# One load moved ahead of two selects, eight small loads moved behind a memset: the start of a fused attention and feed-forward kernel

## The chip, the cores and the metric

The kernel runs on one core of a Trainium2 chip. A core has five engines that work side by side, each through its own queue in order: TensorE (PE in the profile; its weight loads are PEld), VectorE (DVE), ScalarE (ACT), GpSimd (POOL) and SyncE (SP, which only issues DMAs here). ACT, POOL and SP can issue DMAs; the transfers themselves run on 16 DMA engines. The metric is the device time of one execution in microseconds, the median of several runs.

## The reference

Two steps follow one another. The first is causal attention with a window of 128 positions and 4 sink positions that every query sees; the second is a layer norm and a two-layer feed-forward net with a residual. The inputs q, k, v have the shape (4, 8, 768, 64) in float32, the weights 512 x 2048 and 2048 x 512; the output is (4, 768, 512) in float32.

```python
scores = scale * np.matmul(q, k.transpose(0, 1, 3, 2))
keep = is_sink | in_window            # pos < 4, or 0 <= q_pos - k_pos < 128
a = softmax(np.where(keep, scores, -1e9))
x = heads_side_by_side(np.matmul(a, v))          # (4, 768, 512)
xn = (x - mu) / np.sqrt(var + 1e-06) * g_ln
out = x + np.maximum(xn @ w_ch1, 0.0) @ w_ch2
```

## The kernel before, in words

The 3072 rows are 24 tiles of 128 rows; two tiles are a chunk, so there are 12 chunks, three for each of the four batches. For each chunk the kernel loads q and k, brings them into transposed form (`kq`), computes scores, takes the exponential on ACT, masks, multiplies with v (`vn`), normalises on VectorE (`rec`, `x`, `st`, `xc`), transposes `xc` into `xnt`, and runs the two layers on PE (lines 873 and 880 for the first, 911 and 960 for the second).

The order of the work is not written out by hand and not left to a scheduler at run time. Every operation is recorded with `P.op(name, engines, priority, emit, ...)`; `Plan.run` (lines 113 to 195) goes through them with an assumed duration for each, and the result, sorted by planned start, is the order in which the instructions are emitted on every engine. `prio` decides among operations that are ready; `nb` is a time before which an operation isn't planned. Neither is a wait on the chip: there an engine takes its next instruction as soon as the semaphores of the data it reads or overwrites allow. Behind the plan, lines 1061 to 1080 fill gaps that the plan leaves on PE in the first 24 us with matmuls of a tile named `junk`, which keep PE busy and whose results nobody reads (line 1085).

The constants are recorded with `constant(...)`. The ones that matter here: `idf0` and `up0` are memsets on VectorE of `ident_f` and `upper`; `idf1` and `up1` are two `affine_select` instructions on POOL (lines 460 and 463) that make the identity and the triangle of them. VectorE then casts `ident` (466), makes `neg` from the triangle (492 to 494), and `sel`, `pick` and `mask` (498 to 507). `neg` is what PE adds into the scores of tiles 0 and 1 in place of a mask (line 701); `ident` is what PE transposes with. `vc0` (497) fills `vc`, a constant for the sinks' v.

The loads at the start:
- chunk 0, tile 0: q and k, four DMAs in float32 into `n4a`, issued by SP and ACT (line 593). VectorE and ACT cast them (610), PE transposes (622), ACT and VectorE evict into `kq` (568).
- chunk 0, tile 1: k and q, one DMA each, issued by POOL (line 599), transposed by PE (618).
- after these, on POOL's queue: v of tile 0 (562), k and q of chunk 1 into `n4b` (575), v of tile 1, and the four quarters of the first layer's weights (529) with further v loads between them; then chunk 2 into `n4c` and the second layer's weights (532).
- the sinks' v of all batches: eight DMAs of 4 KB each, one for each head, issued by SP (line 517) into 4 partitions each of `vc`. They read nothing, and write into `vc` after `vc0` has filled it. VectorE makes `vs` of it for the batches 1 to 3 (line 521); batch 0 gets its `vs` in another way (lines 676 and 679).
- g_ln, one small DMA on SP (509).

POOL issues a DMA in about 0.7 to 1 us of its own time, and takes the next instruction of its queue only then. Eight DMAs of POOL can be under way; the ninth waits for the first.

PE transposes chunk 1 from `n4b` in line 645, VectorE and ACT evict it (568).

Of the kernel before, what the change touches and what calls it, by code (L numbers as in the profile page):

```python
# [64 lines left out]
class Plan:  # L65
# [47 lines left out]
    def run(self):  # L113
# [8 lines left out]
        while ready:  # L122
# [5 lines left out]
            for o in ready:  # L128
                if "PE" in o.engs and o is not head and o.prio >= PAR["strict"]:
                    continue  # L130
# [67 lines left out]
def pe(us):  # L198
    return {"PE": (us, us + Plan.PE_DRAIN)}
# [12 lines left out]
def fix(occ, extra=0.09):  # L212
    return (occ, occ + extra)
# [12 lines left out]
NEG = -1e30  # L226
NEVER = -1e9

PAR = dict(split=(3, 4, 5, 6, 7), gsum=-8.0, guard=183.0, strict=40.0, win=0.4, tr=-8.0, sc=-5.3, sc1=-2.0, av=2.0, trx=9.0, by_dma=4, x_by_dma=2, g_on_w=2, av2=20.0, avi=1.0, behind=5, gtt=9.0, ramp=0.3, vs0=2.6, vpb=12.0,
           w1p=(0.15, 1.7, 2.05, 2.8), pm=2, w2p=(4.5, 4.51, 4.52, 4.53), by_tile=2, wino=2, vp=(0.0, 0.1, 2.0, 2.1, 4.2, 4.3), ld1=0.05)  # L230


# [129 lines left out]
def kernel(  # L362
# [59 lines left out]
    def const(name, shape, dtype):  # L422
        return consts.tile(shape, dtype, name=name)
# [6 lines left out]
    vc = const("vc", [128, B, 65], FP32)  # L430
# [15 lines left out]
    Bc = {n: Buf(n) for n in names}  # L446
# [5 lines left out]
    def constant(name, eng, us, prio, emit, reads=(), **kw):  # L452
        return P.op(name, {eng: fix(us)}, prio, emit, reads=[Bc[r] for r in reads], **kw)

    V, G = nc.vector, nc.gpsimd
# [1 line left out]
    constant("up0", "DVE", 0.13, -98, lambda e: V.memset(upper, 1.0), writes=[Bc["upper"]])  # L457
    constant("junk", "DVE", 0.28, -97, lambda e: V.memset(junk, 0.0), writes=[Bc["junk"]])
    constant("tab0", "DVE", 0.06, -96, lambda e: V.memset(one_e, 1.0), writes=[Bc["tab"]])
    constant("idf1", "POOL", 0.3, -99, lambda e: G.affine_select(  # L460
        out=ident_f, in_=ident_f, compare_op=ALU.not_equal, fill=1.0, base=0,
        pattern=[[-1, 128]], channel_multiplier=1), rw=[Bc["ident_f"]])
    constant("up1", "POOL", 0.3, -98, lambda e: G.affine_select(
        out=upper, in_=upper, compare_op=ALU.is_ge, fill=0.0, base=0,
        pattern=[[1, 128]], channel_multiplier=-1), rw=[Bc["upper"]])
    constant("idb", "DVE", 0.2, -90, lambda e: V.tensor_copy(ident, ident_f), ["ident_f"], writes=[Bc["ident"]])
# [1 line left out]
         rw=[Bc["tab"]])  # L468
# [22 lines left out]
    def negs(e):  # L491
# [14 lines left out]
    constant("ones_f", "DVE", 0.06, 7.0, lambda e: V.memset(ones_f, 1.0), writes=[Bc["ones_f"]])  # L506
    constant("masks", "DVE", 0.8, 6.0 if PAR["pm"] == 4 else -20.0, masks, ["upper"], writes=[Bc["mask"]], nb=20.0 if PAR["pm"] == 4 else 0.0)

# [3 lines left out]
    P.op("gtt", pe(0.06), 0.62, lambda e: nc.tensor.transpose(pg.t[:, 0:NDM], g4, ident_f[0:NDM, 0:NDM]),  # L512
         reads=[Bc["g4"], Bc["ident_f"]], writes=[pg], nb=PAR["gtt"])
    P.op("gt", {"DVE": fix(0.08)}, 0.63, lambda e: V.tensor_copy(gt, pg.t[:, 0:NDM]), reads=[pg], writes=[Bc["gt"]])
    for h in range(H):
        p0 = 32 * (h // 2) + NS * (h % 2)
        P.op(f"vcd{h}", {"SP": (0.3, 0.3)}, 3.2 + 0.01 * h, lambda e, h=h, p0=p0: nc.sync.dma_start(
            vc[p0:p0 + NS, :, 0:64], v[:, h, 0:NS, :].rearrange("b s d -> s b d")),
            reads=[Bc["vc"]], writes=[Bc["vcd"]], dma=HW_T, nb=30.0)
# [5 lines left out]

    w1prio = PAR["w1p"]
    for c in range(4):
# [3 lines left out]
    for c in range(4):  # L531
        P.op(f"w2ld{c}", {"POOL": (0.75, 0.8)}, PAR["w2p"][c], lambda e, c=c: G.dma_start(
            w2[c], moe_w_ch2[512 * c:512 * (c + 1), :].rearrange("(t p) n -> p t n", p=128)),
            writes=[Bw2[c]], dma=SW_W)

    def at(c, step):
        return 16.0 * c - 8.0 + PAR[step]

# [590 lines left out]
```

## Time and profile before

Median of three runs: 210.94 us (210.87 to 211.26). The profiled execution is one of its own: 211.71 us, of which the profile shows a span of 210.2 us.

| | us |
|---|---|
| median of the runs | 210.94 |
| profiled execution, span | 211.71, 210.2 |
| PE busy | 203.0 (97% of the span) |
| VectorE busy | 162.2 (77%) |
| ACT busy | 114.1 (54%) |
| POOL busy | 83.5 (40%) |
| first select on POOL starts | 1.36 |
| first load on POOL starts | 1.86 |
| PE starts on chunk 1's transposes | 12.85 |

A line of the profile names an engine, a line of the kernel, and what is written from what. In a timeline or a chain each row begins with the start in microseconds from the beginning of the span and the length; brackets hold the idle time of the engine just before, and what ended it. "SPq" is SyncE's queue of DMAs. In the list of loads the last column is the median time from issue to landing. Busy PE is not PE at its peak, since matmuls overlap.

### The profile page before, as it was taken

What the parts mean: (1) busy time and instruction counts of PE and PEld (TensorE: products, weight loads), DVE (VectorE), ACT (ScalarE), POOL (GpSimd) and SP (SyncE); (2) the same over time, 40 slices, a digit from 0 to 9 for tenths busy, and PEclk for the clock granted to TensorE, in tenths of its full rate; (3) what the DMA queues carried; (4) which work ended last, traced back from release to release, by engine and by line L of the source; (5) the groups of instructions that cost most, each with busy time, mean ns of one, the idle gap of its engine ahead of it and who ended that gap; (6) DMA issues with size and microseconds to landing.
All of it is one profiled execution on the core that took longest, in us unless ns stands there. A gap on an engine that the chain in (4) does not pass through costs nothing.

```text
span 210.2 us, 6259 instructions
## 1 busy us (share of the span) xinstructions
PE 203.0 (97%) x2539; PEld 167.9 (80%) x2544; DVE 162.2 (77%) x410; ACT 114.1 (54%) x168; POOL 83.5 (40%) x126
## 2 busy tenths in 40 slices
PE   6978999999999999999999999999999999999994
PEld 2657997764787997997987987987988988988883
DVE  5579759999688688798687797797787786797353
ACT  2559479837564564564556555554457457450620
POOL 7967583369058057058066066066020020020000
PEclk9999999999999999999999999999999999999999
DMA  5999999999999949939959939939954520220202
GB/s 115 156 198 191 199 191 208 189 173 154 212 167 127 172 109 136 188 78 120 166 122 150 174 79 156 172 77 151 177 100 53 150 53 3 100 50 4 103 30 83
DMA packets 101243, 27.51 MB, mean 131 GB/s; under 512 B 89556, under 2 KB 99032, under 8 KB 101208
## 3 DMA queue, kind: packets, MB, share of 16 engines
q0 software_dynamic: 67712, 13.37, 77.7%
q1 hardware_dynamic: 33208, 13.41, 35.5%
q8 instruction: 21, 0.34, 0.7%
q10 hardware_dynamic: 288, 0.26, 0.4%
q14 instruction: 14, 0.11, 0.2%
HBM read 27.30 MB, written 6.29 MB: 160 GB/s over the span
## 4 chain that ended last, share of the span: by engine, by line
PE 90%; DMA 3%; DVE 3%; POOL 2%; issue 0%; DVEq 0%
PE one L880 33%; PE one L960 30%; PE one L873 7%; PE one L911 7%; PE pair L805 5%; PE pair L763 4%; DMA n4b<-in_q_dram 3%; PE pair L800 2%; PE one L645 1%; POOL nat L599 1%; PE one L767 1%; DVE xnt L857 1%; DVE kq L568 1%; POOL vn L562 0%; DVE st L824 0%
## 5 line engine op out<-in xcount | busy, mean ns | idle before, releaser
L890 ACT ACTIVATE hq<-one 128x512 bf16<-128x512 f32 x92 | 55.0, 597 | 55.7 <-PE one L880 46.7
L880 PE MATMUL one<-xnt,w 128*128 128x256 bf16 x640 | 74.5, 273 | 0.0
L880 PEld LDWEIGHTS <-w 128*128 128x128 bf16 x640 | 61.4, 98 | 7.0
L777 ACT ACTIVATE pe<-pair 128x1024 bf16<-128x1024 f32 (+1 forms) x40 | 36.2, 960 | 23.2 <-PE pair L763 19.0
L832 POOL TENSOR_SCALAR st<-st 128x1 f32<-128x1 f32 x24 | 6.2, 259 | 88.2 <-DVE rec L818 74.6
L960 PEld LDWEIGHTS <-hs 128*128 128x128 bf16 x320 | 30.0, 98 | 5.2 <-DVE tm L974 0.3
L974 DVE TENSOR_TENSOR tm<-one,x 128x256 f32<-128x256 f32 x40 | 16.9, 422 | 12.3 <-PE one L960 12.3
L781 DVE TENSOR_TENSOR pe<-pe,mask 128x1024 bf16<-128x1024 bf16 (+1 forms) x40 | 24.9, 644 | 1.0 <-ACT pe L777 0.8
L960 PEld LDWEIGHTS <-hq 128*128 128x128 bf16 x240 | 23.5, 98 | 2.7
L562 POOL DMA_DIRECT2D vn<-in_v_dram x24 | 21.8, 922 | 2.0 <-DMA w<-in_moe_w_ch_dram 1.1
L943 DVE TENSOR_TENSOR hs<-hq 128x512 bf16<-128x512 bf16 x40 | 15.4, 413 | 5.3 <-ACT hq L890 5.2
L960 PE MATMUL one<-w,hq 128*128 128x256 bf16 x160 | 19.1, 273 | 0.0
L981 DVE TENSOR_TENSOR ot<-one,tm 128x256 f32<-128x256 f32 x40 | 16.7, 418 | 1.1 <-PE one L960 0.9
L820 DVE TENSOR_TENSOR x<-pair,rec 128x512 bf16<-128x512 f32 x24 | 16.6, 691 | 0.8
L824 DVE BATCH_NORM_STATS2 st<-x 128x6 f32<-128x512 bf16 x24 | 16.6, 692 | 0.5
L873 PE MATMUL one<-xnt,w 128*128 128x128 bf16 x256 | 16.3, 219 | 0.5 <-DVE xnt L857 0.5
L873 PEld LDWEIGHTS <-w 128*128 128x128 bf16 x256 | 14.7, 98 | 1.6 <-issue 0.5
L659 POOL DMA_DIRECT2D nat<-in_k_dram x16 | 15.0, 938 | 2.5 <-DMA w<-in_moe_w_ch_dram 2.5
L659 POOL DMA_DIRECT2D nat<-in_q_dram x16 | 14.2, 898 | 3.4 <-DMA w<-in_moe_w_ch_dram 3.4
L833 POOL TENSOR_TENSOR st<-st,mhalf 128x1 f32<-128x1 f32 x24 | 14.2, 592 | 2.0
L911 PE MATMUL one<-w,hq 128*128 128x512 bf16 x60 | 14.8, 380 | 0.2
L805 PE MATMUL pair<-vn,pe 128*128 128x65 bf16 x352 | 14.6, 193 | 0.0
(113 smaller groups left out, 245.1 us busy)
## 6 DMA issues: line engine op xcount, KB each, us to landing
out_dram<-ot SPq DMA_DIRECT2D x17, 256.0 KB
w<-in_moe_w_ch_dram POOLq DMA_DIRECT2D x8, 512.0 KB, 12.6
vn<-in_v_dram POOLq DMA_DIRECT2D x24, 128.0 KB, 7.2
nat<-in_k_dram POOLq DMA_DIRECT2D x17, 128.0 KB, 4.8
nat<-in_q_dram POOLq DMA_DIRECT2D x17, 128.0 KB, 5.3
out_dram<-ot SPq DMA_DIRECT2D x14, 128.0 KB
kq<-nat SPq DMA_TRANSPOSE x32
xnt<-xc SPq DMA_TRANSPOSE x20
```

What stands on the lines that cost most here:

```text
L562: P.op(f"vld{t}", {"POOL": (0.87, 0.9)}, prio, lambda e: G.dma_start(bv.t[:, :, 0:64], v[b, :, 128 * r:128 * (r + 1), :].rearrange("h p d ...
L659: lambda e, nat=nat, ap=ap: G.dma_start(nat.t, ap), writes=[nat], dma=SW, after=behind(c))
L777: P.op(f"ex{c}{hp}", {"ACT": act(2 * n)}, d + 0.1 + 0.05 * j, lambda e, pp=pp, pb=pb: nc.scalar.activation(pb.t[:, :, 0:n], pp.t[:, :, 0:n ...
L781: V.tensor_mul(pb.t[:, :, 0:n], pb.t[:, :, 0:n], mm),
L805: nc.tensor.matmul(po.t[:, h // 4, 65 * (h % 4):65 * (h % 4) + 65], lhsT=part(h, n), rhs=vn_b[tv].t[:, h, :], start=(not R and h % 4 == 0 ...
L873: nc.tensor.matmul(ph.t[:, 128 * s:128 * s + 128], lhsT=w1[u // 2][:, j, 128 * s:128 * s + 128], rhs=xnt.t[:, j, 128 * (u % 2):128 * (u % ...
L880: nc.tensor.matmul(ph.t[:, 256 * s:256 * s + 256], lhsT=w1[ht // 4][:, j, 128 * (ht % 4):128 * (ht % 4 + 1)], rhs=xnt.t[:, j, :], start=j ...
L890: nc.scalar.activation(hg.t[:, u % 4, :], ph.t, AF.Relu)
L911: nc.tensor.matmul(pc.t[:, 0:wd], lhsT=(hq[s // 2].t[:, (2 * s + i) % 4, 128 * ii:128 * ii + 128] if by_tile else hq[ht // 8].t[:, ht // 2 ...
L960: nc.tensor.matmul(at(r), lhsT=get(left, g)[:, v, s, :], rhs=rhs, start=first and n == 0, stop=n == 7, skip_group_check=True)
L974: return P.op(f"tm{name}_{c}", {"DVE": dve(256, 1.14)}, pr, lambda e: V.tensor_tensor(tm[name].t, at(r), xs[i].t[:, sl], op=ALU.add), read ...
L981: return P.op(f"o{c}_{half}", {"DVE": dve(256, 1.14)}, pr, lambda e: V.tensor_tensor(ots[i].t[:, sl], at(r), tm[name].t, op=ALU.add), read ...
```

## The change

Two constants on POOL, the identity's and the triangle's select, get a later priority, so that the plan puts the k load of tile 1 ahead of them on POOL's queue. The q load of tile 1 and all else on POOL stay behind them. A new constant `vc1` on VectorE sets one column of `vc` for batch 0 to zero (it is zero already, and nobody reads it). It is planned for 26 us at the earliest. Since it writes `vc`, the eight sink loads, which write `vc` too and are recorded behind it, wait for it on SP.

```diff
-PAR = dict(split=(3, 4, 5, 6, 7), ...
+PAR = dict(idf=-49.95, vc1=7.0, vc1nb=26.0, split=(3, 4, 5, 6, 7), ...
...
-    constant("idf1", "POOL", 0.3, -99, lambda e: G.affine_select(
+    constant("idf1", "POOL", 0.3, PAR["idf"], lambda e: G.affine_select(
         out=ident_f, in_=ident_f, compare_op=ALU.not_equal, fill=1.0, base=0,
         pattern=[[-1, 128]], channel_multiplier=1), rw=[Bc["ident_f"]])
-    constant("up1", "POOL", 0.3, -98, lambda e: G.affine_select(
+    constant("up1", "POOL", 0.3, PAR["idf"] + 0.01, lambda e: G.affine_select(
         out=upper, in_=upper, compare_op=ALU.is_ge, fill=0.0, base=0,
         pattern=[[1, 128]], channel_multiplier=-1), rw=[Bc["upper"]])
...
+    constant("vc1", "DVE", 0.06, PAR["vc1"], lambda e: V.memset(vc[:, 0, 0:1], 0.0), rw=[Bc["vc"]], nb=PAR["vc1nb"])
     for h in range(H):
         p0 = 32 * (h // 2) + NS * (h % 2)
         P.op(f"vcd{h}", {"SP": (0.3, 0.3)}, 3.2 + 0.01 * h, lambda e, h=h, p0=p0: nc.sync.dma_start(
```

What the plan makes of it, engine by engine. POOL: the k load stands ahead of the two selects and of the library instruction before them; nothing else moves. VectorE: the cast of `ident` moves behind the memsets of `vn` and `kts`, and the memsets of `vc`, `mhalf` and `ones_f` move ahead of it and of `neg`; the new memset stands behind `xc` of tile 3 and ahead of the eviction of tile 3's `xnt`. PE: ahead of the `neg` matmuls of tile 0 stand one 512-column and one 128-column `junk` matmul more, behind them one of each fewer. SP and ACT: the same instructions in the same order; the first of the eight sink loads waits for the new memset instead of the old one.

More of the change, by code (lines that the diff above doesn't have):

```diff
@@ L227 @@
 NEVER = -1e9
-PAR = dict(split=(3, 4, 5, 6, 7), gsum=-8.0, guard=183.0, strict=40.0, win=0.4, tr=-8.0, sc=-5.3, sc1=-2.0, av=2.0, trx=9.0, by_dma=4, x_by_dma=2, g_on_w=2, av2=20.0, avi=1.0, behind=5, gtt=9.0, ramp=0.3, vs0=2.6, vpb=12.0,
+PAR = dict(idf=-49.95, vc1=7.0, vc1nb=26.0, split=(3, 4, 5, 6, 7), gsum=-8.0, guard=183.0, strict=40.0, win=0.4, tr=-8.0, sc=-5.3, sc1=-2.0, av=2.0, trx=9.0, by_dma=4, x_by_dma=2, g_on_w=2, av2=20.0, avi=1.0, behind=5, gtt=9.0, ramp=0.3, vs0=2.6, vpb=12.0,
            w1p=(0.15, 1.7, 2.05, 2.8), pm=2, w2p=(4.5, 4.51, 4.52, 4.53), by_tile=2, wino=2, vp=(0.0, 0.1, 2.0, 2.1, 4.2, 4.3), ld1=0.05)
```

## The prediction

> **What bounds the kernel now.** I read the busy table first: PE is busy 203.0 of 210.2 us (97%), and the granted clock is 1.00 in every stretch. So from the moment PE's stream is unbroken the time is PE's own work, and a change of the constants and first loads can only move the moment at which that stream begins. The chain that ended last, in order of time, shows what sets that moment (columns: start, length, what):
>
> ```profile
> 1.36 0.29 POOL ident_f L460
> 1.65 0.26 POOL upper L463
> 1.91 1.96 POOL nat L599 x2
> ...
> 5.39 7.32 DMA n4b<-in_q_dram
> ...
> 12.85 0.65 PE one L645 x16
> 13.51 0.02 issue
> 13.53 1.22 DVE kq L568
> ...
> 18.20 0.70 DVE xnt L857
> ...
> 18.94 1.99 PE one L873 x32
> ```
>
> The two selects on POOL stand ahead of POOL's queue of loads; the last of the first five, q of chunk 1 into n4b, lands at 12.7 and releases PE's transposes, then VectorE works without a gap to 18.9. Behind 18.94 the chain is PE pieces with a few hundredths of "issue", to VectorE's last addition at 206.99. So what is gained at 12.7 is gained at the end, if VectorE can take it.
>
> How much it can take is in the timelines of PE and VectorE (start, length; in brackets the idle time before and its releaser):
>
> ```profile
> 11.21 0.40 PE L713 MATMUL pair<-kq 64*128 64x128 bf16 x8
> 12.85 1.08 PE L645 MATMUL one<-ident,n4b 128*64 128x128 bf16 x32 [1.25 <-DMA n4b<-in_q_dram]
> ```
> ```profile
> 12.11 0.46 DVE L835 TENSOR_SCALAR xc<-x,st 128x512 bf16<-128x512 bf16 x1
> 13.53 1.22 DVE L568 COPY kq<-one 128x1024 bf16<-128x1024 bf16 x1 [0.96 <-PE one L645]
> ```
>
> PE waits 1.25 us for n4b, VectorE 0.96 us for what PE makes of it. The smaller is the cap: 0.96 us.
>
> The POOL and SP timelines show the instructions that move:
>
> ```profile
> 1.86 1.11 POOL L599 DMA_DIRECT2D nat<-in_k_dram  x1
> 2.96 0.91 POOL L599 DMA_DIRECT2D nat<-in_q_dram  x1
> ```
> ```profile
> 3.54 2.72 SPq L517 DMA_DIRECT2D vc<-in_v_dram  x8
> 43.85 0.38 SPq L923 DMA_DIRECT2D out_dram<-ot  x1
> ```
>
> Loads, issue to landing (last column, us), and the first microseconds by engine (last two columns: DMA share, GB/s):
>
> ```profile
> n4b<-in_k_dram POOLq DMA_DIRECT2D x1, 256.0 KB, 6.7
> n4b<-in_q_dram POOLq DMA_DIRECT2D x1, 256.0 KB, 7.3
> ```
> ```profile
> 3.00:4.00 1.00, 1.00 (x5) 0.44 (x4) 0.89 (x8) 0.44 (x2) 1.00 (x2) 1.00 1.07 341
> 4.00:5.00 1.00, 1.00 (x5) 0.43 (x4) 0.25 (x3) 0.00 (x0) 1.00 (x2) 1.00 0.85 69
> 5.00:6.00 1.00, 1.00 (x4) 0.30 (x2) 0.47 (x1) 0.62 (x1) 1.00 (x2) 1.00 2.08 135
> 6.00:7.00 1.00, 1.00 (x14) 0.81 (x13) 0.00 (x0) 0.16 (x1) 1.00 (x3) 1.00 2.25 149
> ```
>
> Issue plus landing gives 6.66 (k, tile 1), 7.46 (q), 8.84 (v), 11.4 (n4b k), 12.7 (n4b q), 13.7 (v, second), 16.05 (first w1 quarter). POOL issues them 0.7 to 0.9 apart, so from about 5 us the transfers are behind the issuing. But at 4 to 5 us only 69 GB/s move: chunk 0's own loads are nearly done, and POOL's first load has barely begun.
>
> **The change part by part.** *The k load ahead of the selects.* POOL's last start-up memset ends at 0.72, and SP's and ACT's first loads start at 1.02, so k's issue goes from 1.86 to about 1.02: 0.84 earlier. It lasts 1.11, to 2.13. Then come the library instruction of line 460 (unseen in the timeline; it lies before 1.36 now, so between 0 and 0.34; I take 0.1) and two selects 0.25 apart. q's issue starts at 2.73 instead of 2.96, and every later issue is 0.23 earlier.
>
> *What that does to n4b.* The stream can move by 0.23 (only the issuing) up to 0.84 (as much as its first load). I take 0.7, near the upper end: the row of 4 to 5 us is a hole that k's 128 KB fit into (0.9 us at the 135 to 149 GB/s of the next two rows), and behind it the loads queue. The Trainium skill (DMA: Bandwidth & Descriptors, section Issuing engines are not separate DMA queues) speaks against this: loads of all engines run on the same 16 DMA engines and interleave, and an earlier start saves only issue time; by it the term is 0.23, the second rival below.
>
> *k beside chunk 0's loads.* k's packets now run while the 0.5 MB of n4a on SP and ACT are moving. n4a can land later by nothing up to 0.9 (all of k in front). The casts of line 610 start at 5.17 and end at 5.79; the transposes that need them start at 6.42 behind warm-up matmuls, a cover of 0.6. Above it, tile 0's chain (evictions, scores, x, xc at 12.11) slips and eats the cap: up to 0.3. I take 0.1.
>
> *Identity and triangle later.* They end at 2.48 and 2.73 instead of 1.65 and 1.9. VectorE's neg needs 2.17 to 3.23 now, about 1.3 behind the triangle: it ends at 4.0. PE's neg matmuls start at 3.97 today, behind five 512-column and one 128-column warm-up matmuls. The new order has one more of each ahead (2.42 us for the six today; some 0.43 + 0.11 more) and one of each fewer behind: 4.5, so neg is 0.5 early, and the transposes stay at 6.4. VectorE's masks, last of its constants, end at 4.25 today and near 4.5; the cast comes at 5.2. Cost nothing; if POOL's selects end over 0.5 later than I reckon, tile 0's chain pays the excess.
>
> *The eight v loads.* Out of 3.54 to 6.26, behind a one-column memset, which the new order puts behind VectorE's xc of tile 3 (27.21 to 27.56) and ahead of an instruction that waits 1.07 us for PE: its 0.06 costs nothing. SP has nothing between 6.3 and 43.85, where the first store of a result waits; eight issues of 0.34 end near 30, so nothing queues behind them. Their reader, line 521, first runs at 48.2. If that cover were gone, each late microsecond would stand on VectorE ahead of chunk 4. What they free early: at least their 32 KB at 160 GB/s, 0.2 us; at most 1.3, the excess of n4b k's landing behind its forerunner (11.4 - 8.84 = 2.6) over n4b q's (1.3), in the stretch in which they are in flight. I take 0.3, near the lower end, since n4b k follows loads of smaller packets and may be slow without them. The Trainium skill (DMA: Bandwidth & Descriptors, section Why a DMA increments its semaphore by 16 and not by 1) says that a load whose slowest dimension is 4 runs on 4 of the 16 engines; each would then do 32 of the 128 packets, and as an estimate at this page's 36 ns a packet (35.5% of 16 x 210.2 us over 33208) the term is 1.2 there. No view shows single engines.
>
> *What they collide with later.* At 28 to 33 us the second layer's first quarter is in flight: it lands at 32.4, PE's first use is at 34.0. 0.2 to 1.3 against a slack of 1.6: nothing.
>
> *Sum.* n4b q lands 0.7 + 0.3 = 1.0 earlier, at 11.7. PE is free at 11.6, starts at 11.85, and VectorE's copy could start at 12.53; it is free at 12.57. The cap binds: 0.96. Less 0.1 for tile 0: 0.86. What could be late next: the second v (13.7; its use at 14.11 becomes 13.3) is part of the same stream and moves to 12.7; the first w1 quarter (16.05 against 16.80) needs at least 0.2 of the stream's 1.0; the third (22.0 against 22.64) 0.3. All hold. Gain 0.85 us, on the profiled execution 211.71 (span 210.2) to 210.86. That execution lies 0.77 above the median of the runs, 210.94, so in the median it is **210.1**.
>
> **The rivals.** *Only the issue time is gained.* If the DMA engines share k and n4a out of one capacity, n4b moves by the 0.23 of POOL's queue alone: 210.7. For it: 341 GB/s at 3 to 4 us, already a full rate. Against: the 69 GB/s that follow. *Tile 0 becomes the bound*: n4a lands a whole 0.9 later, or neg comes late by the same amount above its slack: gain 0.6, and with both near 0.2, 210.3 to 210.8. *The identity and triangle come much too late* (the other side): place, PE's neg matmuls; price, one for one above 0.5 us of slack. Tile 0's xc then ends late by d, and VectorE's copy starts at 12.57 + d; at d = 0.96 all gain is gone and at 1.4 the kernel is slower by over 0.2%. That needs POOL's selects to end 1.9 us later than I reckon, at 4.6. At 2.5 us later it is 212.0. For it: k's first issue is the longest of POOL's (1.11), and the library instruction behind a load is not shown before. Against: selects and loads change over without a gap at 1.86, and later rows of line 832 start 0.07 us behind a load.
>
> **How the numbers follow.** Forecast 0.60 (210.1, own range 209.8 to 210.5); issue time only 0.17 (210.7); tile 0 the bound 0.09 (a third of it still a gain of over 0.2%); identity late or another loss 0.14. A run tells 0.2%, or 0.42 us, from no change. Faster 0.63, same 0.23, slower 0.14. The range leaves out the late identity: low is the cap with nothing lost and 0.2 for spread, 209.75; high is no gain and as much, 211.15.
>
> **What would show it.** After: POOL's k issue near 1.0, q's near 2.7; the 4 to 5 us row well above 69 GB/s; n4b q landing before 12; line 645 near 11.8 with hardly a wait; VectorE's 0.96 gone; the 32 w1 matmuls at 18.0 to 18.2; SP's eight loads at 27 us and no new wait at 43. Wrong if line 610 starts past 5.8, if line 701 starts past 4.6, or if PE waits for a w1 or w2 quarter after 16 us.

## The result, and the profile after

The changed kernel takes 211.56 us in the median (211.11 to 212.38, 12 runs). The kernel before, run beside it, takes 211.19 (210.76 to 211.59, 12 runs). The ratio is 1.0024, with an interval of 1.0013 to 1.0036. The change costs about 0.4 us (0.37 by the medians, 0.5 by the ratio), where 0.85 had been forecast as a gain. The forecast of 210.1 lies below every run of the changed kernel, and the upper end of the range, 211.15, only just above the fastest.

One thing has to be known before the two profiles are compared. The profiled execution of the changed kernel took 211.11 us and is the fastest of its 12. The profiled execution of the kernel before, 211.71, lies above all 12 runs of that kernel that were timed beside it. So the two traces taken alone say "0.6 faster", and the runs say "0.4 slower". What can be read from a pair of traces here is where instructions stand and how long each takes on its engine. When a load lands is another matter, as will be seen.

The chain that ended last, changed kernel (start, length, what; lines behind 514 have moved down by one):

```profile
0.92 0.61 issue
...
1.55 1.09 POOL nat L600
2.65 0.08 POOLq L460 x2
...
2.75 0.32 POOL ident_f L460
3.06 0.24 POOL upper L463
3.30 0.85 POOL nat L600
...
5.98 6.26 DMA n4b<-in_q_dram
...
12.37 0.65 PE one L646 x16
...
18.46 1.99 PE one L874 x32
```

The same load ends the start-up as before: q of chunk 1 into `n4b`. What lies ahead of it is now POOL's queue nearly without a gap. The first row is new: 0.61 us in which POOL waits for nothing that the profile shows, and then the k load begins at 1.55. Behind k, the row of POOL's sequencer (2.65, 0.08) is the library instruction, and the two selects follow.

The timeline of POOL, changed kernel (start, length; in brackets the idle time before and what ended it), and below it the last two of these loads in the kernel before, which were not shown yet:

```profile
1.55 1.10 POOL L600 DMA_DIRECT2D nat<-in_k_dram  x1 [0.82 <-POOLq L1111]
2.75 0.32 POOL L460 TENSOR_SCALAR_AFFINE_SELECT ident_f<-ident_f 128x128 f32<-128x128 f32 x1
3.00 0.30 POOL L463 TENSOR_SCALAR_AFFINE_SELECT upper<-upper 128x128 bf16<-128x128 bf16 x1
3.24 0.91 POOL L600 DMA_DIRECT2D nat<-in_q_dram  x1
4.15 0.88 POOL L563 DMA_DIRECT2D vn<-in_v_dram  x1
5.01 0.97 POOL L576 DMA_DIRECT2D n4b<-in_k_dram  x1
5.98 0.69 POOL L576 DMA_DIRECT2D n4b<-in_q_dram  x1
```

```profile
4.72 0.71 POOL L575 DMA_DIRECT2D n4b<-in_k_dram  x1
5.39 0.72 POOL L575 DMA_DIRECT2D n4b<-in_q_dram  x1
```

k starts 0.31 earlier than before (1.55 for 1.86), not 0.84. q starts at 3.24, 0.28 later than before (2.96), not 0.23 earlier. And the issue of k into `n4b` takes 0.97 where it took 0.71, so q of `n4b` starts at 5.98 for 5.39: 0.59 later.

What stands beside that issue, and beside the one of v ahead of it, is in the timeline of VectorE, changed kernel first, then the kernel before:

```profile
4.28 0.17 DVE L494 MEMSET neg<- 4x128 uint32 x1
...
4.42 0.63 DVE L502 COPY pick<-ident 128x128 bf16<-128x128 bf16 x1
4.51 0.67 DVE L481 COPY mask<-upper 128x512 bf16<-128x512 bf16 x1
5.11 0.27 DVE L482 TENSOR_SCALAR mask<-upper 128x512 bf16<-128x512 bf16 x1
...
13.05 1.23 DVE L569 COPY kq<-one 128x1024 bf16<-128x1024 bf16 x1 [0.61 <-PE one L646]
26.91 0.06 DVE L515 MEMSET vc<- 128x1 f32 x1
28.03 0.69 DVE L858 TENSOR_TENSOR xnt<-one,gt 128x512 bf16<-128x512 bf16 x1 [1.06 <-PE one L844]
```

```profile
3.65 0.24 DVE L502 COPY pick<-ident 128x128 bf16<-128x128 bf16 x1
3.75 0.29 DVE L481 COPY mask<-upper 128x512 bf16<-128x512 bf16 x1
3.96 0.29 DVE L482 TENSOR_SCALAR mask<-upper 128x512 bf16<-128x512 bf16 x1
```

The copies of `pick` and `mask` take 0.63 and 0.67 us for 0.24 and 0.29. The last of them ends at 5.18 for 4.04. For the most part they run beside POOL's issue of v (4.15 to 5.03), which keeps its length; beside the issue that grows, k of `n4b` from 5.01, stand the last 0.17 of the `mask` copy and the second `mask` instruction (5.11, 0.27), which keeps its own. The new one-column memset costs what was said, 0.06 in front of a wait of 1.06.

PE's, ACT's and SP's timelines, changed kernel:

```profile
4.50 1.33 PE L702 MATMUL pair<-neg,ident 128*128 128x512 bf16 x4
6.00 0.61 PE L623 MATMUL one<-ident,hq 128*128 128x128 bf16 x8
...
12.37 1.08 PE L646 MATMUL one<-ident,n4b 128*64 128x128 bf16 x32 [1.13 <-DMA n4b<-in_q_dram]
```

```profile
5.03 0.62 ACT L611 CAST hq<-n4a 128x512 bf16<-128x512 f32 x1 [1.58 <-DMA n4a<-in_q_dram]
```

```profile
27.01 2.67 SPq L518 DMA_DIRECT2D vc<-in_v_dram  x8
43.25 0.38 SPq L924 DMA_DIRECT2D out_dram<-ot  x1
```

The `neg` matmuls start at 4.50 without a wait and tile 0's transposes at 6.00, 0.4 earlier than the 6.4 of before: PE's work on tile 0 isn't late. The first cast of chunk 0 starts at 5.03 for 5.17, so `n4a` isn't later either; VectorE's half of the casts, behind its masks, starts at 5.30 for 5.21. The eight sink loads stand at 27.01 and the store behind them at 43.25, with no new wait. PE still waits 1.13 us for `n4b`.

The load that ends the wait (last column: us from issue to landing) and the first stretches (last two columns: DMA share, GB/s), changed kernel:

```profile
n4b<-in_q_dram POOLq DMA_DIRECT2D x1, 256.0 KB, 6.3
```

```profile
4.00:5.00 1.00, 1.00 (x6) 0.45 (x5) 0.92 (x5) 0.00 (x0) 1.00 (x2) 1.00 2.00 140
5.00:6.00 1.00, 1.00 (x8) 0.49 (x7) 0.71 (x4) 0.62 (x1) 1.00 (x3) 1.00 1.33 85
6.00:7.00 1.00, 1.00 (x14) 0.64 (x11) 0.18 (x1) 0.58 (x2) 1.00 (x2) 1.00 1.70 108
```

The load takes 6.3 us to land in this execution, for 7.3. The hole at 4 to 5 us is filled, 140 GB/s for 69, as was forecast. But the next two rows fall, from 135 and 149 to 85 and 108: the hole has moved behind k, to where q and v are issued later. The two other traces of the changed kernel show the same more weakly: 97 and 114 GB/s at 4 to 5 us, then 116 and 100, and 121 in both.

### The profile page after: what moved, and what is told of

Read it like the earlier page. It is cut to its first block, busy times and chain, and to the rows that moved or that the text cites. A ratio compares the mean times of both kernels' runs of the same rounds, so it can differ in the third digit from the quotient of the medians.

```text
span 209.6 us, 6260 instructions
## 1 busy us (share of the span) xinstructions
PE 202.4 (97%) x2539; PEld 167.8 (80%) x2544; DVE 162.6 (78%) x411; ACT 114.1 (54%) x168; POOL 83.8 (40%) x126
## 4 chain that ended last, share of the span: by engine, by line
PE 90%; DMA 3%; DVE 3%; POOL 2%; issue 1%; POOLq 0%; DVEq 0%
PE one L881 33%; PE one L961 30%; PE one L874 7%; PE one L912 7%; PE pair L806 5%; PE pair L764 4%; DMA n4b<-in_q_dram 3%; PE pair L801 2%; PE one L646 1%; POOL nat L600 1%; PE one L768 1%; DVE xnt L858 1%; DVE kq L569 1%; POOL vn L563 0%; DVE st L825 0%
## 5 line engine op out<-in xcount | busy, mean ns | idle before, releaser
L975 DVE TENSOR_TENSOR tm<-one,x 128x256 f32<-128x256 f32 x40 | 16.8, 421 | 12.4 <-PE one L961 12.3
```

What stands on the lines that cost most here:

```text
L975: return P.op(f"tm{name}_{c}", {"DVE": dve(256, 1.14)}, pr, lambda e: V.tensor_tensor(tm[name].t, at(r), xs[i].t[:, sl], op=ALU.add), read ...
```

## The experiments

The letters in the expectations: T1 says that the loss is POOL's queue, because the selects now stand between two loads and k's load has a preparation that the trace doesn't show, so q and `n4b` are issued later. T2 says that the loss is in the late sink loads. C says that VectorE's late copies, which hold up the issue of `n4b`'s k, have a share of their own, and Q that only the place on the queue counts. V with a number stands for what the early sink loads may cost.

The runs come in three groups, each with the kernel before beside it; its medians there were 211.34 (35 runs), 211.25 (35) and 211.42 (29). Each ratio is against the kernel before of the same group.

**One part of the change at a time.** The changed kernel once more:

> The changed kernel once more, for a second trace and as the measure of the three others. Both theories expect +0.2 to +0.6 us against the kernel before. Theory T1 (POOL's queue): the k load starts near 1.55 and not 1.02, q near 3.24 (2.96 before), and n4b's q load is issued near 6.0 (5.39 before) in this trace too. Theory T2 (the sink loads at 27 us): POOL's rows may do as they like; PE waits for a second-layer quarter between 34 and 43 us.

211.65; ratio 1.0028 (1.0008 to 1.0048). The loss stands, and k, q and `n4b`'s q start at 1.54, 3.24 and 5.97, as T1 says. Then only the k load ahead of the selects, the sink loads as before:

```diff
-PAR = dict(split=(3, 4, 5, 6, 7), ...
+PAR = dict(idf=-49.95, vc1=7.0, vc1nb=26.0, split=(3, 4, 5, 6, 7), ...
...
-    constant("idf1", "POOL", 0.3, -99, lambda e: G.affine_select(
+    constant("idf1", "POOL", 0.3, PAR["idf"], lambda e: G.affine_select(
...
-    constant("up1", "POOL", 0.3, -98, lambda e: G.affine_select(
+    constant("up1", "POOL", 0.3, PAR["idf"] + 0.01, lambda e: G.affine_select(
```

> Only the first half of the change: the k load ahead of the selects; the sink loads stay at 3.5 us. T1: slower than before by 0.4 to 1.0 us, at least as slow as the whole change, since the sink loads' part is a gain or nothing. T2: no slower than before (within 0.2 us), or faster. The prediction as it was put expected a gain of 0.6 to 0.85.

211.57; 1.0018 (0.9999 to 1.0038): 0.23 us by the medians, 0.38 by the ratio, a little less than the 0.4 to 1.0 that T1 expected. And only the late sink loads, the selects first as before:

```diff
-PAR = dict(split=(3, 4, 5, 6, 7), ...
+PAR = dict(idf=-99, vc1=7.0, vc1nb=26.0, split=(3, 4, 5, 6, 7), ...
...
+    constant("vc1", "DVE", 0.06, PAR["vc1"], lambda e: V.memset(vc[:, 0, 0:1], 0.0), rw=[Bc["vc"]], nb=PAR["vc1nb"])
```

> Only the second half: the selects stay ahead, the sink loads wait for the memset at 27 us. T1: faster than before by 0.1 to 0.6 us; the slowest share of n4b's k load lands within 0.5 us of the one before it (1.36 us before). T2: slower than before by 0.4 us or more, with a wait of PE for second-layer quarters.

211.24; 0.9991 (0.9976 to 1.0006). Once more, in the second group:

> The kernel with only the sink loads late, once more, to narrow its interval and for a second trace. T1 as it stands after the first four runs: 0 to 0.3 us faster than before (0.9985 to 1.0); PE's 32 w1 matmuls start 6.2 us behind the landing of n4b's q load. If the sink loads' move costs something after all, it is slower than before.

211.21; 1.0001 (0.9980 to 1.0022). So the gain of 0.1 to 0.6 that T1 gave the late sink loads isn't there either. The last share of `n4b`'s k lands 0.02 us behind the one before it in the first of the two traces, as expected, but 0.62 behind it in the second; and with k first alone, where the sink loads are early, it is 0.06. So the late last share of the kernel before, 1.36, doesn't go with the sink loads.

The loss goes with k's new place: without the late sink loads it is there in size, though that interval just reaches 1, and with them alone it is not. T2 falls: it asked for a loss of 0.4 us with them alone, and for a wait of PE for weights, and in the changed kernel's trace PE waits for no weights between 16 and 50 us. POOL's timeline with k first alone is that of the changed kernel:

```profile
1.54 1.10 POOL L599 DMA_DIRECT2D nat<-in_k_dram  x1 [0.82 <-POOLq L1110]
...
5.97 0.69 POOL L575 DMA_DIRECT2D n4b<-in_q_dram  x1
```

**No sink loads at all.** If moving the loads frees nothing, taking them out should free nothing. The sinks' v of the batches 1 to 3 then stays zero: that part of the computation is left out.

```diff
-    for h in range(H):
-        p0 = 32 * (h // 2) + NS * (h % 2)
-        P.op(f"vcd{h}", {"SP": (0.3, 0.3)}, 3.2 + 0.01 * h, lambda e, h=h, p0=p0: nc.sync.dma_start(
-            vc[p0:p0 + NS, :, 0:64], v[:, h, 0:NS, :].rearrange("b s d -> s b d")),
-            reads=[Bc["vc"]], writes=[Bc["vcd"]], dma=HW_T, nb=30.0)
```

> The kernel before without the eight sink loads, so the sinks' values are zero in batches 1 to 3 and its output there is not the reference's. Theory V0 (the eight loads cost next to nothing wherever they stand): within 0.2 us of before and of the kernel with late sink loads. Theory V1 (early they cost, late they don't): as fast as the kernel with late sink loads, 0.1 to 0.4 us below before. Theory V2 (late they cost as much as early): 0.2 us or more below the kernel with late sink loads.

211.33; 1.0004 (0.9982 to 1.0026). Nothing is freed that could be measured. In this trace k of `n4b` lands at 11.22, behind v at 9.08, a distance of 2.1 us with no sink load in flight; with k first alone, where they are in flight, it is 0.9. So the slow landing from which the prediction read its 1.3 (2.6 less 1.3) doesn't go with the sink loads.

**The same delay without the change.** To measure what queue time on POOL costs by itself, two selects on a spare tile were put between the k and the q load of the kernel before; the real ones stay in front. The tile's memset also puts 0.14 us on VectorE:

```diff
+    spare, sb_ = const("spare", [128, 128], FP32), Buf("spare")
+    P.op("sp0", {"DVE": fix(0.13)}, -95, lambda e: V.memset(spare, 0.0), writes=[sb_])
+    for i in range(2):
+        P.op(f"sp{i + 1}", {"POOL": fix(0.3)}, -49.95 + 0.01 * i, lambda e: G.affine_select(
+            out=spare, in_=spare, compare_op=ALU.not_equal, fill=1.0, base=0,
+            pattern=[[-1, 128]], channel_multiplier=1), rw=[sb_])
```

> The kernel before, with two selects on a spare tile put between the k load and the q load on POOL's queue; nobody reads the tile, and the identity and the triangle come as early as before. T1: what costs is that two selects stand behind the first load: q is issued 0.5 later, n4b's q at 5.9, and the kernel is slower than before by 0.3 to 0.5 us, about as slow as k_first. A theory by which the later identity and triangle cost expects no change; one by which the loads are behind the issuing by so much that 0.5 us on the queue is hidden expects less than 0.1 us.

211.91; 1.0035 (1.0012 to 1.0057): 0.66 us more than the kernel before. POOL's timeline of this kernel:

```profile
1.85 1.11 POOL L605 DMA_DIRECT2D nat<-in_k_dram  x1
2.97 0.68 POOL L469 TENSOR_SCALAR_AFFINE_SELECT spare<-spare 128x128 f32<-128x128 f32 x2
3.60 0.92 POOL L605 DMA_DIRECT2D nat<-in_q_dram  x1
...
6.06 0.71 POOL L581 DMA_DIRECT2D n4b<-in_q_dram  x1
```

q of `n4b` is issued at 6.06, 0.67 later than in the kernel before, and the time is 0.66 longer by the medians (the ratio's interval is 0.25 to 1.2), where T1 had put 0.3 to 0.5. The issue of k into `n4b` keeps its 0.70 here. Queue time of POOL ahead of `n4b` goes through to the end. That is T1's mechanism, shown without the change.

**One select ahead, one behind.** The identity's select stays in front of k and fills POOL's start, the triangle's goes behind k; the sink loads are late:

```diff
-PAR = dict(split=(3, 4, 5, 6, 7), ...
+PAR = dict(idf=-49.95, vc1=7.0, vc1nb=26.0, split=(3, 4, 5, 6, 7), ...
...
     constant("idf1", "POOL", 0.3, -99, lambda e: G.affine_select(
...
-    constant("up1", "POOL", 0.3, -98, lambda e: G.affine_select(
+    constant("up1", "POOL", 0.3, PAR["idf"] + 0.01, lambda e: G.affine_select(
...
+    constant("vc1", "DVE", 0.06, PAR["vc1"], lambda e: V.memset(vc[:, 0, 0:1], 0.0), rw=[Bc["vc"]], nb=PAR["vc1nb"])
```

> The identity's select stays ahead of the k load, only the triangle's goes behind it; the sink loads late as in the change. T1: POOL has about 0.5 us of its own to spend before the first load whatever stands there, so one select ahead of it costs nothing: k starts near 1.6, q near 2.95 as before, and the time is that of the kernel with late sink loads alone within 0.2 us. A theory by which the later identity is what costs expects the same time here; one by which the later triangle costs expects the time of the whole change.

211.41; 1.0014 (0.9996 to 1.0032). Neither better nor clearly worse than the kernel before, and 0.17 above the late sink loads alone, within the 0.2 that T1 gave; the triangle as the cause would have put it at the changed kernel's 211.65, which the interval doesn't rule out. The expected q near 2.95 was missed. POOL's timeline, and VectorE's beside it:

```profile
1.36 0.29 POOL L460 TENSOR_SCALAR_AFFINE_SELECT ident_f<-ident_f 128x128 f32<-128x128 f32 x1 [0.63 <-DVE ident_f L456]
1.71 1.11 POOL L600 DMA_DIRECT2D nat<-in_k_dram  x1
2.82 0.32 POOL L463 TENSOR_SCALAR_AFFINE_SELECT upper<-upper 128x128 bf16<-128x128 bf16 x1
3.07 0.92 POOL L600 DMA_DIRECT2D nat<-in_q_dram  x1
3.97 1.26 POOL L563 DMA_DIRECT2D vn<-in_v_dram  x1
```

```profile
4.26 0.28 DVE L481 COPY mask<-upper 128x512 bf16<-128x512 bf16 x1
4.47 0.27 DVE L482 TENSOR_SCALAR mask<-upper 128x512 bf16<-128x512 bf16 x1
```

k starts at 1.71, 0.15 earlier than in the kernel before, and q at 3.07, 0.11 later. The surprise is the issue of v: 1.26 us, where it takes 0.88 to 0.91 in the other kernels. VectorE's two `mask` instructions run beside it, and this time they keep their length and POOL's issue is the one that grows.

**The masks taken off VectorE.** The changed kernel with the two `mask` instructions on ACT, which is idle there:

```diff
-        V.tensor_copy(blocks(mask, 1), up)
-        V.tensor_scalar(blocks(mask, 0), up, -1.0, 1.0, op0=ALU.mult, op1=ALU.add)
+        nc.scalar.copy(blocks(mask, 1), up)
+        nc.scalar.activation(blocks(mask, 0), up, AF.Copy, bias=1.0, scale=-1.0)
...
-    constant("masks", "DVE", 0.8, ...
+    constant("masks", "ACT", 1.2, ...
```

> The changed kernel, with the two mask operations of lines 481 and 482 on ACT in place of VectorE, so that they don't run on VectorE while POOL issues n4b's k load. Theory C (VectorE's late copies hold up POOL's issue): n4b's k issue takes 0.7 us again (0.97 in the change), the q issue follows at 5.7 instead of 6.0, and the time is 0.1 to 0.3 us below the changed kernel's. Theory Q (only the place on the queue counts): the issue still takes 0.97 and the time is that of the changed kernel.

211.29; 1.0003 (0.9980 to 1.0025). Again in the third group, beside the changed kernel as it is:

> The changed kernel with the two mask operations on ACT, beside the changed kernel itself. Theory C (VectorE's late copies hold up POOL's issue of n4b's k load by 0.26): at least 0.15 us below the changed kernel, and 0 to 0.2 over before. Theory Q (only the place on POOL's queue counts): the changed kernel's time within 0.1 us.

> The changed kernel a third time, as the measure on the same chip for the two that follow: 0.2 to 0.5 us over before.

With the masks on ACT 211.50, 1.0007 (0.9993 to 1.0022); as it is 211.52, 1.0017 (0.9999 to 1.0036). POOL's timeline in the first and in the second of the two runs with the masks on ACT:

```profile
5.01 0.71 POOL L576 DMA_DIRECT2D n4b<-in_k_dram  x1
5.71 0.69 POOL L576 DMA_DIRECT2D n4b<-in_q_dram  x1
```

```profile
5.02 0.78 POOL L576 DMA_DIRECT2D n4b<-in_k_dram  x1
5.79 0.69 POOL L576 DMA_DIRECT2D n4b<-in_q_dram  x1
```

The issue of k is back at 0.71 and 0.78, with the selects, k and q where they were. So it was the two `mask` instructions that made it 0.97; the copy of `pick` stayed on VectorE, beside v's issue, and takes 0.64 in both traces. On the issue C was right and Q wrong. What this is worth in time is not settled: where both kernels ran side by side their medians differ by 0.02 us, as Q said and not the 0.15 of C, over all groups by about 0.3 (below), and the intervals overlap.

**Late sink loads and masks on ACT, selects first**, to see whether the two harmless parts together beat the kernel before (the edits of the two diffs above, with `idf=-99`):

> The control: the selects ahead of the k load as before, sink loads late, and the two mask operations on ACT. If the masks on ACT gain by themselves, it lies 0.15 us or more below before; by theory C they gain only where they stand beside n4b's issue, and it lies within 0.15 us of before, with n4b's q load issued at 5.4.

211.46; 1.0003 (0.9992 to 1.0013). They don't. No version that ran beats the kernel before by an amount that these runs can tell.

**All profiled executions together.** Start of the issue of `n4b`'s q, its landing, the start of the 32 w1 matmuls (line 873 before), and what is left to the execution's own time, in us:

| kernel | time of this execution | issued | landed | w1 matmuls | time less that |
|---|---|---|---|---|---|
| before | 211.71 | 5.39 | 12.72 | 18.94 | 192.77 |
| changed | 211.11 | 5.98 | 12.24 | 18.46 | 192.65 |
| changed, again | 211.69 | 5.97 | 12.61 | 18.83 | 192.86 |
| changed, third | 211.52 | 5.98 | 12.60 | 18.82 | 192.70 |
| k first alone | 211.38 | 5.97 | 12.29 | 18.52 | 192.86 |
| late sinks alone | 210.53 | 5.39 | 11.50 | 17.73 | 192.80 |
| late sinks alone, again | 210.83 | 5.39 | 12.02 | 18.23 | 192.60 |
| no sink loads | 212.32 | 5.38 | 12.80 | 19.02 | 193.30 |
| spare selects | 211.89 | 6.06 | 12.96 | 19.18 | 192.71 |
| one select ahead | 211.56 | 5.89 | 12.49 | 18.71 | 192.85 |
| masks on ACT | 211.26 | 5.71 | 12.35 | 18.57 | 192.69 |
| masks on ACT, again | 211.10 | 5.79 | 12.24 | 18.46 | 192.64 |
| late sinks, masks on ACT | 211.46 | 5.37 | 12.60 | 18.82 | 192.64 |

In all 13 the w1 matmuls start 6.21 to 6.23 us behind the landing, and but for one row the rest takes 192.6 to 192.9 (in the row without sink loads the chain also waits for a w1 quarter that lands at 26.7). So the landing of one load sets the time of these kernels. And that landing is noisy. Three executions that issue the load at 5.37 to 5.39, from their chains:

```profile
5.39 6.12 DMA n4b<-in_q_dram
```

```profile
5.39 6.63 DMA n4b<-in_q_dram
```

```profile
5.37 7.23 DMA n4b<-in_q_dram
```

The first two are the same kernel (late sinks alone), the third has the masks on ACT as well. The landings are 11.50, 12.02 and 12.60: half a microsecond apart within one kernel, and 1.1 over the three, in which POOL's queue is the same. That is more than all that the change does.

The medians over all runs are what can be compared. Each run was set against the median of the kernel before in its own group (for 12 of the changed kernel's, the runs of the result), and the interval was found by drawing the runs anew 2,000 times:

| kernels | runs | q of `n4b` issued later by | time against before |
|---|---|---|---|
| late sinks (three kernels) | 35 | 0 | -0.06 (-0.16 to 0.07) |
| changed, masks on ACT | 24 | 0.32 and 0.40 | 0.03 (-0.06 to 0.27) |
| changed | 36 | 0.59 | 0.31 (0.11 to 0.53) |
| k first alone | 12 | 0.58 | 0.23 (-0.06 to 0.55) |
| one select ahead | 12 | 0.50 | 0.07 (-0.23 to 0.60) |
| no sink loads | 12 | 0 | 0.08 (-0.09 to 0.53) |
| spare selects | 12 | 0.67 | 0.66 (0.38 to 0.88) |

## Why the prediction was wrong

**What bounds the start-up: right.** It is the landing of `n4b`'s q, and what moves it moves the end: the 6.2 us from it to the w1 matmuls are the same in all 13 executions, and the 192.6 to 192.9 behind these in 12.

**"So k's issue goes from 1.86 to about 1.02": this is the step that failed.** It took POOL to be ready 0.3 us behind its last start-up memset, because SP's and ACT's first loads start at 1.02. POOL's first load starts at 1.55 in every kernel that puts it first. About 0.6 us ahead of it (the chain's "issue" from 0.92 to 1.52) go to something the trace doesn't name. In the kernel before, the two selects run from 1.36 to 1.9, the first of them begins within that same stretch, and the load follows the second without a gap. Nor is it a time that POOL needs in any order: by the trace's records of POOL's sequencer, it goes on to line 460 at 0.98 in the seven traces with a select first, and at 1.52 in the six with the load first. The first select at 1.36 waits only for VectorE's memset of `ident_f`. So the selects cost k 0.31 us, not 0.84. Behind k they have nothing to hide in: 0.50 for the two, and some 0.1 for the library instruction, which was sized right, stand between k and q. From k's 1.55 and its 1.1, q starts at 3.24 instead of the 2.73 forecast. The change takes work out of a cover and puts it on the queue. What POOL does in these 0.6 us, whether it is the first load's own preparation, and whether all of it could be hidden, stays open.

**The masks "cost nothing": wrong, and the second part of the delay.** The prediction asked whether VectorE's late constants delay VectorE, PE or the cast. They hardly do, as it said (VectorE's cast 0.09). It didn't ask what they run beside. In the kernel before they are done at 4.25, ahead of POOL's issue of `n4b`'s k at 4.72. In the changed kernel they end at 5.38, not near the forecast 4.5: the selects end 0.57 later than reckoned, and the copies take longer beside v's issue. The second `mask` instruction therefore falls into the first part of k's issue, and that takes 0.26 longer. So the 0.59 has two halves: k of `n4b` is issued 0.29 later (5.01 for 4.72), and from there to q it is 0.97 for 0.67. The Trainium skill says of this (SBUF — State Buffer, section Who interferes with whom) that VectorE and GpSimd share one pair of ports under an exclusive lock, which `copy` and `tensor_scalar` can take, and that whoever comes second waits. The trace agrees: both sides are seen to lose, the `mask` copy 0.38 beside v's issue in the changed kernel, which ends at 5.03, 0.15 ahead of the copy, and POOL's v issue 0.35 to 0.38 with one select ahead.

**"The stream can move by 0.23 … up to 0.84": the bounds had the wrong side.** No row excluded a loss, and both ends were gains. The hole at 4 to 5 us was there and k filled it, but the queue that is later behind k opened the next one. Something of this term may be real. With the spare selects, where k doesn't move, the 0.67 of delay comes out as 0.66. In the changed kernel 0.59 come out as 0.31, and with the masks on ACT some 0.36 as 0.03: both times about 0.3 less than the delay. That would be what k's earlier start is worth, against the 0.47 (0.7 less 0.23) in the sum. But with one select ahead 0.50 come out as 0.07, though k starts only 0.15 earlier, and by means in place of medians the changed kernel has 0.43 and the masks on ACT 0.11. The intervals are too wide to call this shown.

**"The eight v loads … I take 0.3": nothing of it was found.** Over 35 runs with late sinks the gain is 0.06, by the interval at most 0.16, and without the loads altogether there is none to be seen. The rule of the Trainium skill that put 1.2 on it (DMA: Bandwidth & Descriptors, section Why a DMA increments its semaphore by 16 and not by 1), by having each such load on 4 engines, is not borne out as a cost here. On how many engines these loads ran, no view shows.

**The cap of 0.96, and the base of 211.71.** The sum was read off one execution whose load landed at 12.72. The runs of that kernel have a median near 211.3; less 192.75 and 6.22 that is a landing near 12.4, and VectorE's wait is shorter by as much. With late sinks alone, in the execution whose load landed at 11.50, VectorE waits only 0.30. So the wait was no property of the kernel that a change could collect. It didn't decide the sign, but a third of the cap or more was one late landing: set against the 210.94 on which the forecast was put, 0.77 of the 0.96. And that base, the median of three runs, was low; later medians of the same kernel are 211.19 to 211.42.

**What held.** `n4a` isn't later; the `neg` matmuls start at the 4.5 that was forecast, and tile 0's transposes aren't late. For `neg` that was close: with the selects 0.57 late it ends at 4.45, and of the 0.5 of slack 0.05 is left. The memset, SP's queue and the second layer's first quarter cost nothing. The rival that only issue time is gained had the right mechanism, as the spare selects show, 0.67 of issue for 0.66 of time. It had the sign of the issue time wrong, like the forecast. The Trainium skill (DMA: Bandwidth & Descriptors, section Issuing engines are not separate DMA queues) says that starting loads on several engines saves only the time of initiating them. The spare selects are in keeping with that. The rival on the slow side had its place on PE, where nothing happened, and none of the three signs of being wrong (lines 610 and 701, the weights) came. The loss came from POOL's own queue, which was thought to gain.

How the loss splits between the place on the queue (0.29) and the collision with VectorE (0.30) is not settled by these runs: the collision's share of the issue time is shown, its share of the end isn't resolved.

## What to carry to other kernels

What stands first on a queue may be nearly free: here the first load did not start before 1.55 in any trace, and two selects ahead of it cost it 0.31. Before such work is moved behind the first load, look for a profile row that shows how soon that engine can issue at all, and don't take it from another engine's. Count every microsecond that the queue spends ahead of the load that ends the wait, including what other engines, now later, do to its issues. And where a wait ends on a load, take its length from many executions, and let the bounds of a moved transfer reach below zero.

## What was not expected of the hardware

- A load at the head of POOL's queue starts 0.93 us behind the start of the last start-up memset (0.62 to 1.55), where SP and ACT start theirs at 1.02. A select in front starts at 1.36, when VectorE's memset is done, and a load follows two of them at 1.86 without a gap.
- Where an issue of a load on POOL and a `copy` or `tensor_scalar` on VectorE run at once, one of them can take longer: issues 0.71 to 0.97 and 0.88 to 1.26, copies 0.24 to 0.63 and 0.29 to 0.67. Which one loses changes with the order: the `mask` instructions kept their 0.28 and 0.27 where the issue grew to 1.26, and v's issue kept its 0.88 where the copies grew.
- A load of 256 KB, issued at the same moment behind the same loads of POOL, took 6.1, 6.6 and 7.2 us to land in three executions of two kernels.
